# Attention and a squared-ReLU feed-forward block on one core: both feed-forward products as seven block products instead of eight

## The chip, the core and the metric

The kernel runs on one core of a Trainium2 chip. The metric is device time in microseconds (us) of one execution. A run gives one time, and its profile gives the span of the core, which lies some 2 us below it. In profile lines PE is TensorE's matmul side, PEld its weight loads, DVE VectorE, ACT ScalarE, POOL GpSimd and SP SyncE, which issues most transfers here. `L84` is line 84 of the kernel that was run, so the same operation has other line numbers in another kernel.

## The reference, cut to what matters

```python
# q, k, v: (8 batches, 8 heads, 576 positions, 64), float32; g_norm: (64,)
kv  = np.einsum('bhsd,bhse->bhde', k, v)          # one 64x64 matrix a head
out = np.einsum('bhsd,bhde->bhse', q, kv)
rms = np.sqrt(np.mean(out * out, axis=-1, keepdims=True) + 1e-06)
x   = (out / rms * g_norm)                        # -> (4608 tokens, 512)

h = x @ w_in                                      # w_in:  (512, 2048)
r = np.maximum(h, 0.0)
g = s * (r * r) + b                               # s, b: scalars
return (g @ w_out).astype(np.float32)             # w_out: (2048, 512)
```

Both weights arrive as 8-byte floats, because they are float32 arrays multiplied by a numpy scalar of 8 bytes. The kernel has to bring them to 4 bytes itself. K and V of a pair of batches are needed before any of its tokens can be worked on. There are four pairs of batches.

## The kernel before

It works in 12 tiles of 384 tokens. The weights are loaded in 32 blocks of 128x512, each converted by nine operations on three engines, and stay in on-chip memory. A tile has 16x4 first products, 384 columns wide, and 3x16 second ones, 512 wide. The attention of the next tile stands between first products, one step behind each. K and V are loaded for two heads at a time and multiplied between second products.

```python
    def round_w(i):                    # 8-byte words -> float32, one block of 512
        raw = w_raw.pop(i).rearrange("p (n two) -> p n two", two=2)
        lo, hi = raw[:, :, 0], raw[:, :, 1]
        ...
        nc.vector.tensor_scalar(out=m, in0=hi, scalar1=0xFFFFF, ...)           # mantissa
        nc.vector.tensor_scalar(out=e, in0=hi, scalar1=20, scalar2=0x7FF, ...)  # exponent
        nc.scalar.activation(l, lo, AF.Copy, scale=2.0**-52)
        nc.scalar.activation(one_m, m, AF.Copy, bias=1.0, scale=2.0**-20)
        nc.vector.tensor_scalar(out=e, in0=e, scalar1=896.0, scalar2=1151.0, ...)
        nc.vector.tensor_scalar(out=e, in0=e, scalar1=896.0, scalar2=2.0**23, ...)
        nc.vector.scalar_tensor_tensor(e, hi, 0x80000000, e, ...)
        nc.gpsimd.tensor_tensor(out=one_m, in0=one_m, in1=l, op=ALU.add)
        nc.gpsimd.tensor_tensor(out=w_sb[i], in0=one_m, in1=e.bitcast(FP32), op=ALU.mult)

    def mm1(T, f):
        h = ps_h.tile([P, N], FP32, name="h_ps", tag="h")
        for c in range(KC):
            nc.tensor.matmul(
                h, lhsT=w_in(c, f), rhs=xT[T][:, c, :], start=(c == 0), stop=(c == KC - 1)
            )
        ...                            # relu on ScalarE, square and s*r^2+b on VectorE

    def mm2(T, j):
        o = ps_o.tile([P, DM], FP32, name="o_ps", tag="o")
        for f in range(FC):
            nc.tensor.matmul(o, lhsT=gT[T, f][:, j * P : j * P + P], rhs=w_out(f), ...)
        ...                            # copied and stored

    # main loop, cut
    for T in range(NT):
        ...
        for f in range(FC):
            if T == 0:
                w_step(f + 2)          # converts a block, loads a later one
            mm1(T, f)
            if f < len(steps):
                steps[f]()             # attention of the next tile
        if T == 0:
            for i in range(FC + 2, 2 * FC):
                w_step(i)              # most of w_out
            ...
        for j in range(J):
            mm2(T, j)
            ...                        # kv_product of the next pair of batches
```

## Time and profile before

| | before |
|---|---|
| time, median of three runs | 1276.54 us (1275.0 to 1276.94) |
| span of the profiled run | 1273.7 us |
| TensorE busy | 1141.2 us, 90% |
| VectorE busy | 408.3 us, 32% |
| end of the first tile | 245.21 us |
| a later tile without K/V products | 92.75 us |

The busy row and the slices (40 equal parts of the span, each digit a busy share in tenths) are shown in the prediction. TensorE is full from the eighth slice on, so the kernel has two parts: a first tile that is held by the conversion of the weights, and eleven tiles that are held by TensorE. In the timeline the columns are start, length and what ran, and in brackets the wait before it. In rows of the page, as the prediction shows them, what stands behind the last bar is idle time before such an instruction, with the instruction that ended it.

```profile
171.56 2.08 PE L294 MATMUL o_ps<-w,gT 128*128 128x512 f32 x2 [2.29 <-POOL w L148]
...
215.19 30.18 PE L294 MATMUL o_ps<-w,gT 128*128 128x512 f32 x66 [2.20 <-POOL w L148]
245.21 2.74 PE L277 MATMUL h_ps<-xT,w 128*128 128x384 f32 x8
```

The second product of the first tile waits some 2.3 us for each block that GpSimd delivers, and GpSimd in turn waits for VectorE's `w_e` (1.62 us here). VectorE has next to no idle time, but its queue is not long by its work alone. Of its 160 conversion operations in the timeline, the 113 that run beside nothing of GpSimd's for more than 0.34 us take at most 0.69 us. The other 47, like the two shown, overlap a GpSimd operation by 1.08 us or more and take 1.37 to 1.67. At the short durations the 125.4 us of VectorE's conversion would be about 76 (an estimate: 32 blocks of 0.42, 0.42, 0.43, 0.43 and 0.69 us). So some 49 us go with running beside GpSimd. That is read from this trace; no run takes GpSimd away by itself.

### The profile page before, as it was taken

The page shows a single profiled execution, that of the slowest core. Times are in us where ns is not written, and L with a number is a line of the kernel's source. Part 1 is how long each engine was busy: PE and PEld are TensorE (multiplying, and loading weights), DVE is VectorE, ACT ScalarE, POOL GpSimd, SP SyncE. Part 2 cuts the span into 40 slices and gives each one's busy share as a digit, 9 for nine tenths or more (in the row PEclk, how much of TensorE's full clock was granted, in tenths as well). Part 3 has the DMA queues.
Part 4 walks back from the last instruction along what each step waited for, and adds up shares of the span by engine and source line. Part 5 has one row for each costly group of instructions (what it writes and reads, how often), then busy time and mean ns, then how long its engine had stood idle before and what let it go on. Part 6 is the DMA issues. An engine that isn't in the chain of part 4 may idle for free.

```text
span 1273.7 us, 11355 instructions
## 1 busy us (share of the span) xinstructions
PE 1141.2 (90%) x4704; PEld 600.7 (47%) x4704; DVE 408.3 (32%) x697; ACT 208.8 (16%) x409; POOL 90.6 (7%) x72
## 2 busy tenths in 40 slices
PE   3576645989999989999989999999999999999998
PEld 3343311455554454454554454454554554554553
DVE  0599996041141041141141141140240140240220
ACT  0233321021021020120120120120120120120110
POOL 0244564000000000000000000000000000000000
PEclk9988755999999999999999999999999999999999
DMA  9223235001620000001610000001410000000000
GB/s 230 51 83 100 97 118 152 21 1 46 146 58 9 16 1 9 17 1 46 170 33 9 17 1 8 17 1 46 105 25 8 17 1 9 16 1 17 9 0 25
DMA packets 63668, 55.27 MB, mean 43 GB/s; under 512 B 40576, under 2 KB 48768, under 8 KB 63616
## 3 DMA queue, kind: packets, MB, share of 16 engines
q1 hardware_dynamic: 57984, 45.10, 14.0%
q10 hardware_dynamic: 5632, 9.44, 2.0%
q8 instruction: 37, 0.61, 0.2%
q14 instruction: 15, 0.12, 0.0%
HBM read 45.09 MB, written 9.44 MB: 43 GB/s over the span
## 4 chain that ended last, share of the span: by engine, by line
PE 75%; DVE 17%; issue 6%; ACT 2%; POOL 0%; POOLq 0%; DVEq 0%
PE o_ps L294 38%; PE h_ps L277 31%; DVE gT L285 3%; PE x_ps L236 2%; DVE w_e L141 2%; DVE w_e L138 2%; DVE r L283 2%; DVE w_e L132 2%; DVE xn L255 2%; DVE ss L249 2%; PE xT_ps L262 2%; ACT r L281 1%; PE kv_ps L196 1%; PE qT_ps L227 1%; DVE w_e L144 1%
## 5 line engine op out<-in xcount | busy, mean ns | idle before, releaser
L294 PE MATMUL o_ps<-w,gT 128*128 128x512 f32 x1152 | 517.0, 608 | 37.8 <-POOL w L148 37.8
L277 PE MATMUL h_ps<-xT,w 128*128 128x384 f32 x1536 | 533.0, 499 | 9.9 <-POOL w L148 9.9
L277 PEld LDWEIGHTS h_ps<-xT,w 128*128 128x128 f32 x1536 | 290.2, 195 | 202.2 <-issue 22.1
L294 PEld LDWEIGHTS o_ps<-w,gT 128*128 128x128 f32 x1152 | 220.6, 194 | 325.4 <-issue 260.2
L283 DVE TENSOR_TENSOR r<-r 128x384 f32<-128x384 f32 x192 | 106.7, 556 | 616.2 <-ACT r L281 616.1
L281 ACT ACTIVATE r<-h_ps 128x384 f32<-128x384 f32 x192 | 93.9, 489 | 354.3 <-PE h_ps L277 337.0
L285 DVE TENSOR_SCALAR gT<-r,s_col,b_col 128x384 f32<-128x384 f32 x192 | 105.6, 550 | 7.9
L302 ACT COPY o_sb<-o_ps 128x512 f32<-128x512 f32 x36 | 21.1, 585 | 477.2 <-PE o_ps L294 477.2
L262 PE MATMUL xT_ps<-ident,xn 128*128 128x128 f32 x144 | 26.3, 311 | 53.9 <-DVE xn L255 53.9
L209 DVE COPY bd_kv<-kv_ps 64x256 f32<-64x256 f32 x8 | 3.4, 423 | 163.5 <-PE kv_ps L196 163.5
L262 PEld LDWEIGHTS xT_ps<-ident,xn 128*128 128x128 f32 x144 | 16.9, 153 | 75.3 <-DVE xn L255 68.8
L147 POOL TENSOR_TENSOR w_1m<-w_1m,w_l 128x512 f32<-128x512 f32 x32 | 43.7, 1366 | 82.3 <-ACT w_1m L137 82.3
L236 PE MATMUL x_ps<-bd_kv,qT 128*64 128x128 f32 x576 | 42.0, 291 | 6.8 <-DVE qT L229 6.8
L148 POOL TENSOR_TENSOR w<-w_1m,w_e 128x512 f32<-128x512 f32 x32 | 45.0, 1405 | 41.6 <-DVE w_e L144 40.0
L236 PEld LDWEIGHTS x_ps<-bd_kv,qT 128*64 128x64 f32 x576 | 32.9, 144 | 26.1 <-issue 16.0
L196 PE MATMUL kv_ps<-v_sb,k_sb 64*64 64x64 f32 x1152 | 25.3, 244 | 19.6 <-DMA v_sb<-in_v_dram 19.6
L196 PEld LDWEIGHTS kv_ps<-v_sb,k_sb 64*64 64x64 f32 x1152 | 22.7, 156 | 27.6 <-issue 22.7
L137 ACT ACTIVATE w_1m<-w_m 128x512 f32<-128x512 uint32 x32 | 20.2, 630 | 92.2 <-DVE w_m L129 92.2
L141 DVE TENSOR_SCALAR w_e<-w_e 128x512 uint32<-128x512 uint32 x32 | 32.2, 1005 | 1.1
L265 ACT ACTIVATE xT<-xT_ps,g_col 128x512 f32<-128x512 f32 x36 | 24.7, 686 | 42.1 <-PE xT_ps L262 42.1
L132 DVE TENSOR_SCALAR w_e<-w_raw 128x512 uint32<-128x512 uint32 x32 | 28.8, 901 | 0.0
L138 DVE TENSOR_SCALAR w_e<-w_e 128x512 uint32<-128x512 uint32 x32 | 26.9, 841 | 1.1
(21 smaller groups left out, 221.6 us busy)
## 6 DMA issues: line engine op xcount, KB each, us to landing
k_sb<-in_k_dram SPq DMA_DIRECT2D x32, 288.0 KB, 4.7
v_sb<-in_v_dram SPq DMA_DIRECT2D x32, 288.0 KB, 5.9
q_sb<-in_q_dram SPq DMA_DIRECT2D x72, 128.0 KB, 3.3
out_dram<-o_sb ACTq DMA_DIRECT2D x36, 256.0 KB, 2.0
w_raw<-in_moe_w_in_dram SPq DMA_DIRECT2D x16, 512.0 KB, 3.7
w_raw<-in_moe_w_out_dram SPq DMA_DIRECT2D x16, 512.0 KB, 3.2
g_col<-in_g_norm_dram ACTq DMA_DIRECT2D x2, 0.2 KB, 3.0
s_col<-in_moe_s_dram ACTq DMA_DIRECT2D x1, 0.5 KB, 5.5
```

The source lines that it names most:

```text
L132: nc.vector.tensor_scalar(out=e, in0=hi, scalar1=20, scalar2=0x7FF, op0=ALU.logical_shift_right, op1=ALU.bitwise_and,)
L138: nc.vector.tensor_scalar(out=e, in0=e, scalar1=896.0, scalar2=1151.0, op0=ALU.max, op1=ALU.min)
L141: nc.vector.tensor_scalar(out=e, in0=e, scalar1=896.0, scalar2=2.0**23, op0=ALU.subtract, op1=ALU.mult)
L148: nc.gpsimd.tensor_tensor(out=w_sb[i], in0=one_m, in1=e.bitcast(FP32), op=ALU.mult)
L196: nc.tensor.matmul(kv_ps[g][s][l * HB : l * HB + HB, p, :], lhsT=kt[rows, l, j, :], rhs=vt[rows, l, j, :], start=(j == 0), stop=(j == R - 1),)
L236: nc.tensor.matmul(st["x"][half, p, :], lhsT=st["qT"][:, p, half], rhs=bd[:, s, p, :], start=True, stop=True,)
L262: nc.tensor.transpose(ps[:, p, :], st["xn"][:, 2 * p : 2 * p + 2, :], ident)
L277: nc.tensor.matmul(h, lhsT=w_in(c, f), rhs=xT[T][:, c, :], start=(c == 0), stop=(c == KC - 1))
L281: nc.scalar.activation(r, h, AF.Relu)
L283: nc.vector.tensor_mul(r2, r, r)
L285: nc.vector.tensor_scalar(out=gT[T, f], in0=r2, scalar1=s_col, scalar2=b_col, op0=ALU.mult, op1=ALU.add)
L294: nc.tensor.matmul(o, lhsT=gT[T, f][:, j * P : j * P + P], rhs=w_out(f), start=(f == 0), stop=(f == FC - 1),)
```

## The change

Its intent is to do seven eighths of the multiplications. A 2x2 block product needs eight block multiplications, or seven with sums of blocks before and after (Strassen's scheme, in a form with few sums). In the new kernel:

- A unit is 512 tokens, so there are 9 units. Both dimensions that are cut in half on each side give 256-column instructions instead of 384 or 512.
- The first product runs in four strips of hidden units. A strip has seven block products of four matmuls. Several of them accumulate into one PSUM bank, and the state in the middle is copied out by ScalarE (`keep`).
- The second product has 14 block products of eight matmuls. The sums of w_out's blocks are not kept on chip: its seven operands, 1 MB each, are made once, **stored to device memory** and streamed back in every unit through a ring of three buffers.
- The conversion of the weights is new: two multiplications on ScalarE, then a shift, a three-operand step and one integer add on VectorE, and nothing on GpSimd.
- `b` is taken out of `g` and comes back as a row, `b` times the column sums of w_out, in the output.
- K and V are loaded one head at a time, and the four head pairs of a pair of batches are multiplied in one run, in the second half of a unit.

The diff, cut to its core (cuts marked "..."; the sums of x, the other block products and the loads are left out):

```diff
-    J = 3
-    TPG = R // J
-    N = J * P
+    TB = 2 * P
+    U = CH // 4
+    NS = FC // 4
...
+        nc.scalar.activation(hi, hi, AF.Copy, scale=2.0**-112)
+        nc.scalar.activation(lo, lo, AF.Copy, scale=2.0**-29)
+        yb, db = raw.rearrange("p (n two) -> p n two", two=2)[:, :, 1], dst.bitcast(U32)
         nc.vector.tensor_scalar(
...
+            out=db, in0=yb, scalar1=3, scalar2=0x7FFFFFFF,
+            op0=ALU.logical_shift_left, op1=ALU.bitwise_and,
         )
         nc.vector.scalar_tensor_tensor(
-            e, hi, 0x80000000, e, ALU.bitwise_and, ALU.bitwise_or
+            db, yb, 0x80000000, db, ALU.bitwise_and, ALU.bitwise_or
         )
-        nc.gpsimd.tensor_tensor(out=one_m, in0=one_m, in1=l, op=ALU.add)
-        nc.gpsimd.tensor_tensor(out=w_sb[i], in0=one_m, in1=e.bitcast(FP32), op=ALU.mult)
+        nc.vector.tensor_tensor(out=db, in0=db, in1=lo, op=ALU.add)
...
+    def make_w_out(s):
+        up = convp.tile([P, 2, DM], FP32, name="w_up", tag="up")
+        dn = convp.tile([P, 2, DM], FP32, name="w_dn", tag="dn")
+        t = convp.tile([P, 3, 2, HN], FP32, name="w_t", tag="wt")
+        round_w(FC + 2 * s, up)
+        round_w(FC + FC // 2 + 2 * s, dn)
...
+        sub(t1, b12, b11)
...                                         # four column sums into wsum
+        sub(t3, b22, b12)
+        sub(t2, b22, t1)
+        sub(t4, b21, t2)
+        for i, src in ((1, b11), (2, b21), (6, t2), (7, t3), (5, t1), (3, b22), (4, t4)):
+            nc.sync.dma_start(out=w2_dram[i][:, 2 * s : 2 * s + 2, :], in_=src)
...
+        def keep(name, src):
+            st[name] = rp.tile([P, 2, TB], FP32, name=name, tag=name)
+            nc.scalar.copy(st[name], src)
+
+        def x1():
+            st["x"] = bank_of("x", "x")
+            mm1_product(1, u, s, st["x"], True)
+            keep("r1", st["x"])
...
+        def x6():
+            mm1_product(6, u, s, st["x"], False)
+            keep("r2", st["x"])
...
+        def product(i, j, ps, first):
+            for f in range(FC // 2):
+                s, b = divmod(f, 2)
+                matmul(
+                    ps, ga[G_OF[i], s][:, b, j * P : j * P + P], ring[u, i][:, f, :],
+                    first and f == 0, f == FC // 2 - 1,
+                )
...
+            if c % R == 0:
+                todo.append([lambda p=p, g=c // R: kv_product(g, p) for p in range(NP)])
+            todo += [[a] for a in attention(c)]
...
+            if u == 0 and n == m1:
+                for s in range(NS):
+                    make_w_out(s)
+                    send_w()
+                    send_w()
+                tc_late()
+                bias_row()
+                load_w2(0, 0)
+                load_w2(0, 1)
...
+                for m, step in enumerate(todo[done]):
+                    step()
+                    if len(todo[done]) > 1 and m < 2:
+                        for h in (4 + 2 * m, 5 + 2 * m):
+                            load_kv(kv_due[u], h)
```

## The prediction

> **What bounds the kernel now.** I read the page first: busy shares, the 40 slices, then the groups of instructions.
>
> ```profile
> PE 1141.2 (90%) x4704; PEld 600.7 (47%) x4704; DVE 408.3 (32%) x697; ACT 208.8 (16%) x409; POOL 90.6 (7%) x72
> ...
> PE   3576645989999989999989999999999999999998
> ...
> DVE  0599996041141041141141141140240140240220
> ...
> PEclk9988755999999999999999999999999999999999
> ...
> L294 PE MATMUL o_ps<-w,gT 128*128 128x512 f32 x1152 | 517.0, 608 | 37.8 <-POOL w L148 37.8
> L277 PE MATMUL h_ps<-xT,w 128*128 128x384 f32 x1536 | 533.0, 499 | 9.9 <-POOL w L148 9.9
> ```
>
> Two stages show. From slice 8 TensorE is full at full clock and VectorE mostly idle. In slices 3 to 7 VectorE is full or nearly so and TensorE half empty, its clock falling to 5 tenths: the conversion of the 8-byte weights. So TensorE bounds the last 1030 us, the conversion what is before.
>
> There are 12 tiles of 384 tokens: 12x16x4 = 768 first products and 36x16 = 576 second ones. The rows count twice that, so an fp32 product is two instructions. Their means (608, 499) overlap each other; the timeline of TensorE gives the true spacing (start, length, what):
>
> ```profile
> 384.28 10.49 PE L277 MATMUL h_ps<-xT,w 128*128 128x384 f32 x32
> 394.60 41.36 PE L294 MATMUL o_ps<-w,gT 128*128 128x512 f32 x96
> 435.80 2.74 PE L277 MATMUL h_ps<-xT,w 128*128 128x384 f32 x8
> ```
>
> (394.60-384.28)/32 = 322.5 ns for 384 columns, (435.80-394.60)/96 = 429.2 for 512: 0.833 ns a column plus 2.5 ns. The products make 12 x (128x0.3225 + 96x0.4292) = 990 us. This tile began at 343.05 in the same view, so it took 92.75 us, 82.5 of it products; 10.25 is the attention of three chunks of 128 tokens, 3.4 us each, of which 1.07 is a wait for VectorE before the second transpose. At the front the same view has the first tile ending at 245.21, so 245.21 - 92.75 = 152 us is not steady work.
>
> **What the Trainium skill says.** "TensorE: Matmul & The Clock Gate", Part 2 (step by step), says the weights of the next matmul load while this one runs, in a time set by their columns, 128/1.2 = 107 ns. The trace agrees with the overlap: a load is recorded at 190 ns (median), yet both shapes leave only 2.5 ns between matmuls. Part 1 there says a pause of some 3.4 us halves the clock; the trace agrees: at 160 to 200 us, products after waits of 2.30 us are 19.20 of 40 us at a granted 0.50. "VectorE: DVE Perf Modes", the TRN2 errata section, gives an fp32 two-tensor operation of N elements (N+151)/0.96 ns. For 512 that is 691, and the trace has 692 for xn. "PSUM — Partial Sum Buffer", The four PSUM rules, allows a synchronised read in the middle of an accumulation group; the changed kernel does this throughout, and no run here shows it.
>
> **Products.** Strassen needs seven block products for eight. Per unit of 512 tokens the first side is 4 strips x 7 x 4 fp32 products, the second 7 x 2 x 8: 224 products, 448 instructions, each of 256 columns. By the line above each takes 213.3+2.5 = 215.8 ns, above the 190 of a weight load, so loads stay hidden: 96.7 us a unit, 9 x 96.7 = **870 us**, 120 less than 990. (7/8 of 990 would be 866; the shorter instruction loses 4.)
>
> **Attention.** Four chunks go in front (below), 32 beside second products. Each is 1.96 us of matmuls in the timeline (0.44, 1.03, 0.49) plus some 0.5 for waits, as its steps now stand a whole second product (3.45 us) apart: 32 x 2.5 = **80 us**, against 33 x 3.4 = 112.
>
> **Sums on VectorE.** A strip has 9 operations of 512 elements, 9 x 0.69 = 6.2 us against 7x8x0.2158 = 12.1 of products. A unit's second half has 14 small ones, 8 of 512 and the attention's, some 20 of 58 us. Both hidden. The seven 1 MB operands of a unit come in over some 58 us with three buffers, 13 us ahead; at the speed below one takes 4.5. Hidden too.
>
> **K and V.** This I read from the order of the built program: for the second to fourth pair of batches all four head pairs are multiplied in one run, with buffers for the first two. The loads of the other two start only when the first products free them. The windows give what the queue moves (the last two columns, DMA share and GB/s):
>
> ```profile
> 18.00:22.00 4.00, 0.17 (x2) 0.21 (x2) 0.00 (x0) 0.00 (x0) 0.00 (x0) 1.00 1.04 238
> 328.00:332.00 4.00, 4.00 (x10) 1.71 (x9) 0.00 (x0) 0.00 (x0) 0.00 (x0) 1.00 0.92 228
> ```
>
> Two heads of K and V are 1.18 MB, 5.1 us at 232 GB/s, the next two 5.1 more, and 2 of latency: 12.2 us, of which 1.2 is hidden. So 1.2 for the first head pair, 12.2, 1.2 for the last, and about 1.8 for a clock gone cold (a pair takes 2.2 us in the first stage, 1.2 later): 16.4 us instead of 4.9, 3 x 16.4 = **49 us**.
>
> **Front.** Two blocks of weights (2 MB, 9 us at that speed) now load ahead of K and V, so the K/V products end near 33 (30.2 before). ScalarE copies and converts until 40, VectorE converts until 47 (11 us, below) and only then serves the norm. Four chunks chained through one PSUM bank at 5.9 us: the products start at **69** (59 before).
>
> **First products of the first unit.** A pair of blocks of w_in is converted per strip. Each block of 1024 elements has a shift (0.68, from 0.42 for 512), a three-operand step (1.22), and an integer add that the order shows as one instruction of 2048 half-words (an estimate by the same formula, 2.29): 4.2 us, two are 8.4, and four sums 2.8: 11.2. With the 6.2 of the strip VectorE needs 17.4 us where TensorE needs 12.1, for three of four strips, part of it absorbed. Followed by hand, the strips take 58 us instead of 48.3: **+10**, at 127.
>
> **The conversion of w_out.** The new second product needs all of w_out, because each operand is stored to device memory and read back. Until then TensorE has nothing: the attention of the next unit also stands behind. A quarter is 8.4 + 5.5 (eight sums) = 13.9 us of VectorE. Its stores stand ahead of the next raw load in one queue, and the last waits for the last sum; so store, load (1 MB for the first block) and ScalarE's step come after it, 2.5 + 7 + 1.1: 24.5 us a quarter. 2 + 13.9 + 3x24.5 + 9 (stores land, first operand read) = **99 us** with TensorE idle, from 127 to 226. This is the largest term against the change.
>
> Sum: 69 + 10 + 99 + 870 + 80 + 49 + 4 (last sum and store) + 5 (small waits, cold clock) = 1186 of span; measured times lie 3 us above it (1276.54 and 1273.7): **1190 us**, 7% less.
>
> **Rivals.** (a) The 256-column instruction does not hide its load, say 240 ns: 4032 x 24 = 97 us more, 1285, the same. For it: 190 recorded leaves only 26 of room. Against: in the timeline sixteen of the attention's instructions take 1.03 us, 64 ns each, though the page records their loads at 144, so a record is longer than what a load holds up. (b) The first stage is well hidden and the gain is nearly the whole 120 plus attention's 30: near 1110. Against it is the order: nothing stands beside w_out's conversion. (c) The mid-group copies, in one queue on ScalarE with one product (1.73 us) of room, hold up TensorE by 0.3 us in each strip product: 252 x 0.3 = 76 us, 1265. A copy takes 0.585, so there is room for two. (d) Streaming operands stall second products. It needs below 150 GB/s, and 228 was reached beside matmuls.
>
> **Range and chances.** w_out's stage is good to 15 us, front and first strips to 12, K/V to 12, small waits in 63 steady strips and products to 15: together about 28, so 1155 to 1230 with some weight above. Over 2% faster means below 1251; only (a) or (c) gets there: 0.93 faster, 0.06 same, 0.01 slower.
>
> **What would show it.** Matmuls of 256 columns spaced 215.8 ns in the timeline, 4032 of them; a unit near 107 us; TensorE empty some 100 us around 127 to 226 with VectorE in bursts of 14 and DMA between; three gaps of about 11 us inside K/V products; first products at 69. It is wrong if spacing exceeds 225, if the idle stretch is below 80 or above 120, or if waits for ScalarE copies recur in every strip.

## More of the kernel before

Lines of the timeline, of VectorE and GpSimd first and then of TensorE, show how the first part runs and ends.

```profile
161.42 1.34 POOL L148 TENSOR_TENSOR w<-w_1m,w_e 128x512 f32<-128x512 f32 x1 [1.62 <-DVE w_e L144]
161.53 1.52 DVE L132 TENSOR_SCALAR w_e<-w_raw 128x512 uint32<-128x512 uint32 x1
...
162.73 1.44 POOL L147 TENSOR_TENSOR w_1m<-w_1m,w_l 128x512 f32<-128x512 f32 x1
...
163.09 1.37 DVE L138 TENSOR_SCALAR w_e<-w_e 128x512 uint32<-128x512 uint32 x1
```

## The result, and the profile after

The changed kernel is correct and takes **1180.21 us** (median of four runs, 1175.63 to 1181.61; the kernel before in the same rounds 1276.22, 1275.0 to 1276.94). The ratio is 0.9242 with a 95% interval of 0.9216 to 0.9268. A ratio here is the mean time of one kernel's fast runs over that of the other's fast runs of the same rounds, so it is not quite the ratio of the medians. The profiled run is of 1181.61 us, its span 1179.8 us.

The page's busy row and its slices:

```profile
PE 1010.7 (86%) x6050; PEld 869.3 (74%) x6050; DVE 480.9 (41%) x765; ACT 203.4 (17%) x338; POOL 2.5 (0%) x8
...
PE   2588100799978999999979999998699999999998
...
DVE  0469565234431355244414452443044534433541
...
DMA  7434445336133401270245023602350234034022
```

Slices are counted from 0 here; each is 29.5 us. Of VectorE's four nines (slices 2 to 5 before) one is left. In their place TensorE has a hole in slices 4 to 6, and there VectorE is only half busy: a chain, no longer a full engine. Three smaller dents follow, at slices 11, 20 and 27 to 28: the K/V runs. Between them TensorE is full. Rows of the page, and the windows view of one undisturbed unit (columns after the window: length, then busy time of PE, PEld, DVE, ACT and POOL with their counts, granted clock, DMA share, GB/s):

```profile
L84 PE MATMUL x_ps<-w_sb,a 128*128 128x256 f32 x864 | 200.6, 386 | 9.7 <-DMA w_sb<-w 9.7
...
L374 ACT COPY r<-x_ps 128x512 f32<-128x512 f32 x108 | 63.2, 585 | 343.7 <-PE x_ps L84 338.8
```

```profile
402.93:508.52 105.59, 105.32 (x545) 91.25 (x544) 44.48 (x74) 17.98 (x32) 0.00 (x0) 1.00 0.27 90
```

Streamed operands (`w_sb`) cost 9.7 us once, before the very first of them, and nothing later. The copies out of the middle of a group are 585 ns each, and no matmul row of the page names them as what it waited for. The undisturbed unit has TensorE busy for 105.32 of 105.59 us, at full clock.

The spacing of the new instruction is read in TensorE's timeline where block products of eight instructions follow each other without a gap (ten such lines are left out at the dots):

```profile
402.94 1.89 PE L84 MATMUL x_ps<-xT,wa 128*128 128x256 f32 x8
...
421.93 1.89 PE L84 MATMUL x_ps<-xs,ws 128*128 128x256 f32 x8
```

From the first line to the last are 11 products of eight instructions, so (421.93 - 402.94)/88 = 215.8 ns each, as the prediction had it. The hole, in the same view and then with all engines and the transfer queue (`SPq` is the issue of transfers):

```profile
121.57 1.89 PE L84 MATMUL x_ps<-xs,ws 128*128 128x256 f32 x8
201.37 2.07 PE L84 MATMUL b_ps<-wsum,b_sq 128*128 128x512 f32 x2 [77.91 <-DVE wsum L161]
213.13 6.56 PE L84 MATMUL x_ps<-w_sb,a 128*128 128x256 f32 x16 [9.69 <-DMA w_sb<-w]
```

```profile
127.59 1.23 DVE L158 CUSTOM_DVE_ANT_0 w_up<-w_raw,w_up 128x2048 uint16<-128x2048 uint16 x1
...
135.68 1.41 DVE L164 TENSOR_TENSOR w_t<-w_dn,w_t 128x512 f32<-128x512 f32 x2
...
138.99 2.29 SPq L130 DMA_DIRECT2D w_raw<-in_moe_w_out_dram  x4
146.19 1.14 ACT L148 ACTIVATE w_raw<-w_raw 128x1024 f32<-128x1024 f32 x1 [17.94 <-DMA w_raw<-in_moe_w_out_dram]
...
147.36 0.69 DVE L151 TENSOR_SCALAR w_up<-w_raw 128x1024 uint32<-128x1024 uint32 x1 [10.27 <-ACT w_raw L148]
```

These five lines are one quarter of w_out. VectorE finishes the last sum at 137.09, the next raw load is issued only at 138.99, after all seven stores, ScalarE starts on what arrived at 146.19, and VectorE goes on at 147.36. VectorE's first step of a quarter falls at 147.36, 169.35 and 191.39, so a quarter takes 22.0 us, and 10.27 of them VectorE waits for this step alone (in all it is busy for 11.37 of 21.99).

A K/V run, in TensorE's timeline and the queue's:

```profile
341.62 2.58 PE L262 MATMUL kv_ps<-v_sb,k_sb 64*64 64x64 f32 x144
347.92 0.33 PE L262 MATMUL kv_ps<-v_sb,k_sb 64*64 64x64 f32 x2 [3.72 <-DMA v_sb<-in_v_dram]
...
358.18 2.15 PE L262 MATMUL kv_ps<-v_sb,k_sb 64*64 64x64 f32 x66 [1.82 <-DMA v_sb<-in_v_dram]
360.26 2.07 PE L84 MATMUL x_ps<-w_sb,a 128*128 128x256 f32 x4
```

```profile
342.93 1.11 SPq L93 DMA_DIRECT2D k_sb<-in_k_dram  x2
```

The first two head pairs (144 instructions) run in 2.58 us from what was loaded early. The loads of the other two are issued from 342.93 on, when the first pair has freed a buffer: sixteen transfers, the last of which is issued by 354.29, with nothing else between them in that queue. The last of them lets TensorE go on at 358.18. The run takes 360.26 - 341.62 = 18.6 us.

### The profile page after: what moved, and what is told of

Same layout as the page of the kernel before. It is cut to its first block, busy times and chain, and to the rows that moved or that the text cites. A ratio compares the mean times of both kernels' runs of the same rounds, so it can differ in the third digit from the quotient of the medians.

```text
span 1179.8 us, 14111 instructions
## 1 busy us (share of the span) xinstructions
PE 1010.7 (86%) x6050; PEld 869.3 (74%) x6050; DVE 480.9 (41%) x765; ACT 203.4 (17%) x338; POOL 2.5 (0%) x8
## 4 chain that ended last, share of the span: by engine, by line
PE 76%; DVE 10%; SPq 5%; DMA 5%; issue 2%; ACT 2%; DVEq 0%; ACTq 0%
PE x_ps L84 42%; PE y_ps L84 23%; PE z_ps L84 5%; SPq L93 4%; PE x_ps L295 3%; PE xT_ps L320 2%; DVE a L164 2%; DMA w_raw<-in_moe_w_out_dram 2%; PE qT_ps L286 1%; DMA v_sb<-in_v_dram 1%; PE kv_ps L262 1%; DVE wsum L161 1%; DVE xn L312 1%; SPq L220 1%; DVE ss L306 1%
## 5 line engine op out<-in xcount | busy, mean ns | idle before, releaser
L84 PE MATMUL x_ps<-w_sb,a 128*128 128x256 f32 x864 | 200.6, 386 | 9.7 <-DMA w_sb<-w 9.7
L84 PEld LDWEIGHTS x_ps<-w_sb,a 128*128 128x128 f32 x864 | 164.3, 193 | 35.6 <-issue 13.8
L84 PE MATMUL y_ps<-w_sb,a 128*128 128x256 f32 x720 | 162.5, 381 | 0.0
L84 PEld LDWEIGHTS y_ps<-w_sb,a 128*128 128x128 f32 x720 | 135.1, 191 | 17.5 <-issue 0.2
L84 PE MATMUL y_ps<-xs,wb 128*128 128x256 f32 x576 | 136.4, 380 | 0.7 <-DVE a L161 0.7
L84 PE MATMUL x_ps<-xs,ws 128*128 128x256 f32 x576 | 136.2, 379 | 0.0
L84 PEld LDWEIGHTS x_ps<-xs,ws 128*128 128x128 f32 x576 | 109.4, 190 | 15.2 <-ACT r L374 0.4
L84 PEld LDWEIGHTS y_ps<-xs,wb 128*128 128x128 f32 x576 | 109.0, 191 | 15.6 <-DVE a L161 1.1
L362 DVE SCALAR_TENSOR_TENSOR a<-a 128x512 f32<-128x512 f32 x108 | 74.7, 692 | 3.7
L84 PE MATMUL z_ps<-xT,wa 128*128 128x256 f32 x288 | 70.1, 387 | 4.5 <-DVE a L161 4.5
L84 PE MATMUL x_ps<-xT,wa 128*128 128x256 f32 x288 | 69.6, 385 | 0.0
```

The source lines that it names most:

```text
L84: nc.tensor.matmul(o, lhsT=lhsT, rhs=rhs, start=start, stop=stop, skip_group_check=True)
L362: nc.vector.scalar_tensor_tensor(t, t, 0.0, t, ALU.max, ALU.mult)
```

## The experiments

All eleven kernels gave correct results and were timed in three rounds beside the kernel before (median 1276.5 to 1276.8 us in each set), four runs each. Each is faster than the kernel before by far more than its interval, so the question is by how much.

The **theory** is the prediction's ledger: each part of it is to be removed by itself. The **rivals** were that another cost, not named in it, sets the time (spacing, copies, streaming), and that the gain is not Strassen's at all.

### 1. The kernel before with only the new conversion

The change bundles two things. This takes the second alone: the kernel before, with `round_w` replaced.

```diff
-        nc.gpsimd.tensor_tensor(out=one_m, in0=one_m, in1=l, op=ALU.add)
-        nc.gpsimd.tensor_tensor(out=w_sb[i], in0=one_m, in1=e.bitcast(FP32), op=ALU.mult)
+        nc.scalar.activation(hi, hi, AF.Copy, scale=2.0**-112)
+        nc.scalar.activation(lo, lo, AF.Copy, scale=2.0**-29)
...                                  # shift, three-operand step
+        nc.vector.tensor_tensor(out=db, in0=db, in1=lo, op=ALU.add)
```

> The kernel before with nothing but the new rounding of the 8-byte weights (two ScalarE, three VectorE operations, no GpSimd). Theory A: a good part of the gain is not Strassen's but this cheaper conversion. VectorE then needs about 1.8 us a block of 512 instead of some 4.4 to 5.2, the first tile of 384 tokens ends near 165 us instead of 245, the steady tiles stay at 92.75, and the time is near 1196 us. Theory B: the gain is Strassen's; the conversion is hidden for the most part, and the time stays above 1250 us.

Measured: **1206.92 us**, ratio 0.9455 (0.9441 to 0.9469). Its slices and the end of its first tile:

```profile
PE   3498799999999999999999999899999999999998
...
DVE  0389604204303402402411411410420430430320
```

```profile
147.22 28.59 PE L283 MATMUL o_ps<-w,gT 128*128 128x512 f32 x66 [1.54 <-DVE w L137]
175.65 2.74 PE L266 MATMUL h_ps<-xT,w 128*128 128x384 f32 x8
```

The first tile ends at 175.65 instead of 245.21, so 69.6 us, and that is the whole gain of 1276.5 - 1206.9 = 69.6. A later tile without K/V products takes 92.75 us (273.49 to 366.24), as before. So 70 of the 96 us that the full change gains are the conversion's, and everything else together brings 26.7. Theory A was right in kind and missed by 10 us (it had the first tile end at 165 and the time at 1196); where these 10 us lie was not followed up. VectorE's shift, which now has no GpSimd operation beside it, takes 421 ns in all 32 blocks.

### 2. K/V products spread, each ahead of its loads' need

The K/V products leave the run in the second half and go between strip products of the first half, one pair at a time, each pair of loads being issued as soon as a buffer is free.

```diff
-            if c % R == 0:
-                todo.append([lambda p=p, g=c // R: kv_product(g, p) for p in range(NP)])
...
+            if u in kv_due and n in (8, 11, 17, 21):
+                p = (8, 11, 17, 21).index(n)
+                kv_product(kv_due[u], p)
+                if p < 2:
+                    for h in (4 + 2 * p, 5 + 2 * p):
+                        load_kv(kv_due[u], h)
```

> The changed kernel with the K/V products of the second to fourth pair of batches moved from one run in the second half of a unit to four places in its first half, two or more block products apart. Theory A: the three long units (126.2, 124.2, 129.9 us) are long by 63.5 us only because the run waits for loads that it itself releases; spread, each costs its own 4.9 us of matmuls, units become 110.5 us, and the time falls by 49 us to about 1131. Theory B: the loads are what is short, and the wait turns up again at the spread products or at the operands of the second product: above 1160 us.

Measured: **1136.54 us**, ratio 0.8907 (0.8892 to 0.8922), 44 us less than the changed kernel. The second pair's products, in TensorE's timeline:

```profile
297.19 1.28 PE L262 MATMUL kv_ps<-v_sb,k_sb 64*64 64x64 f32 x72
```

72 instructions take 1.28 us with no wait. The first pair still waits for its loads (0.64 and 0.69 us). The three units with K/V take 113.11, 112.60 and 111.49 us, where 110.5 were expected, and are 20.4 us over an undisturbed unit in sum where they were 63.5 over. So the run's waits for loads that it releases itself were what made these units long. The edit does two things at once, though: it spreads the run, and it moves the loads into the half of a unit in which no operand is streamed. No run separates the two.

### 3. The raw loads of w_out ahead of the stores

```diff
         sub(t4, b21, t2)
+        send_w()
+        send_w()
         for i, src in ((1, b11), (2, b21), (6, t2), (7, t3), (5, t1), (3, b22), (4, t4)):
             nc.sync.dma_start(out=w2_dram[i][:, 2 * s : 2 * s + 2, :], in_=src)
...
                     make_w_out(s)
-                    send_w()
-                    send_w()
```

> The changed kernel with the next quarter's raw w_out loads put ahead of this quarter's stores in the queue. Theory A: the 22.0 us of a quarter are 11.4 of VectorE and 10.6 of waiting for loads that stand behind stores; with the loads ahead they run beside the sums and a quarter takes about 15 us (VectorE then waits for the stores of its single buffers), TensorE's idle stretch falls from 90 to about 69 us, and the time to about 1159. Theory B: the queue's volume is the bound (2.1 MB in and 1.8 MB out a quarter), a quarter stays at 20 us or more, and the time above 1172.

Measured: **1159.42 us**, ratio 0.9081 (0.9068 to 0.9095), 20.8 us less than the changed kernel. The issue of the raw loads, and TensorE's wait:

```profile
127.20 4.03 SPq L130 DMA_DIRECT2D w_raw<-in_moe_w_out_dram  x4
```

```profile
180.84 2.07 PE L84 MATMUL b_ps<-wsum,b_sq 128*128 128x512 f32 x2 [59.02 <-DVE wsum L161]
```

The loads go out at 127.20 instead of 138.99, and the wait is 59.02 instead of 77.91, which is 18.9 of the 20.8 us. The Trainium skill, "DMA: Bandwidth & Descriptors", section "Anatomy of one DMA — SWDGE (gpsimd) path", says that transfer engines do not wait on semaphores: the issuing sequencer does, before dispatch. Here SyncE issues: a store whose sum is not ready holds the loads behind it in that sequencer (138.99 against 127.20). In the first quarter the loads went out 17.4 us after the last strip product had started (121.57), now 7.3 (119.93 in this run), so some 10 us were lost to the order. A quarter is now 15.4 to 15.9 us (VectorE's first steps at 123.86, 139.25, 155.01 and 170.86), still over VectorE's own 11.4: that first step now waits 3.8 to 4.0 us for a store out of the single buffers. The transfers are hardly faster. They move up to 368 GB/s here, and the changed kernel itself reaches 325 in the same stage (windows view, 142 to 146 us). What changed is that the loads now run beside VectorE's sums and not after them.

### 4 and 5. Strassen's scheme on the first product only

Here the second product is the plain one, 512 columns wide, with w_out resident and nothing stored or streamed.

```diff
-        for i, src in ((1, b11), (2, b21), (6, t2), (7, t3), (5, t1), (3, b22), (4, t4)):
-            nc.sync.dma_start(out=w2_dram[i][:, 2 * s : 2 * s + 2, :], in_=src)
+        for half in range(2):
+            t = wp.tile([P, 2, DM], FP32, name=f"wo_{half}_{s}")
+            round_w(FC + half * (FC // 2) + 2 * s, t)
+            wo[half, s] = t
...
+                    matmul(
+                        st[c], g[:, b, j * P : j * P + P], wo[half, s][:, b],
+                        s == 0 and half == 0 and b == 0, s == NS - 1 and half == 1 and b == 1,
+                    )
```

> Strassen on the first product alone: the second is plain, 512 columns wide, from a w_out that stays on chip, with no operands stored and read back. Theory A: the second product's Strassen saves 9 x 6.6 = 59 us of matmuls and costs nearly all of the 90 us in which TensorE waits for its operands; plain, units take 112.2 us instead of 105.6, but the first unit ends near 206 us instead of 277, and the time is about 1163, below the changed kernel. Theory B: the conversion of w_out holds up TensorE as long without the stores: about 1235 us.

Measured: **1191.73 us**, ratio 0.9335 (0.9318 to 0.9353): a miss, and through faults of the experiment. To make room, single buffers had been given to the kept copies, so TensorE waited for ScalarE (7.75 and 5.72 us), and the column sums stood before the first output and held it for 11.21 us. A third wait for ScalarE, 0.73 us in each of the nine units, has another cause: with the slots changed, the last strip's `x3` follows `x5` directly, with no product between them to cover the copy. The run says nothing about the question. It was built again with two buffers for two of the three kept copies (the transposed q and the normalised x made single for that), and with the sums and the first output later. The wait of some 0.7 us a unit stayed:

> first_only again without its two faults, which its trace shows: single buffers for two kept partial sums (TensorE waited 7.8, 5.7 and eight times 0.7 us for ScalarE copies) and the column sums of w_out in front of the first output (TensorE waited 11.2 us for them). Theory A: that is what put it at 1191.7 instead of 1163; now the first unit ends near 203 us, units take 112 us, and the time is 1151 us, some 29 below the changed kernel: Strassen on the second product, as built, costs more than it saves. Theory B: the plain second product is as slow for another cause: above 1175.

Measured: **1170.79 us**, ratio 0.917 (0.9148 to 0.9192). That lies between the two expectations. Its undisturbed units take 112.62 us, as expected (7.04 over 105.59: 64 second products of 0.858 us instead of 112 of 0.432, 6.6 us by the spacings; the rest is of the size of the 0.68 us for which the copy that no product covers holds TensorE). But the first unit ended at 215.97 instead of 203:

```profile
129.09 6.61 PE L84 MATMUL x_ps<-wo,a 128*128 128x512 f32 x8 [5.13 <-DVE wo L158]
...
151.00 5.92 PE L84 MATMUL x_ps<-wo,a 128*128 128x512 f32 x8 [6.11 <-DVE wo L158]
```

The second product waits for each pair of converted blocks. The quarters came 9.5 to 12.5 us apart, not the 6.3 that VectorE needs for two blocks. In the trace ScalarE's first step waits for the transfer at one place (5.34 us) and stands behind the attention's own operations at another, and no run separates the two. Against the changed kernel the first unit is 60.8 us shorter, the seven middle units and the last are 7x7.04 + 7.6 = 56.9 longer, and K/V runs 10 shorter. So **Strassen's scheme on the second product, as built, is a wash**: what it saves in eight units it spends on its operands in the first. The other 10 us suggest that the streamed operands lengthen the K/V runs in the shared queue (their excess here is 17.4, 17.7 and 18.1 us, against 20.6, 18.6 and 24.3), but that is a comparison and not an isolated run.

### 6 and 7. The mends together

The sixth kernel joins experiments 2 and 3 and moves the column sums of w_out from VectorE to TensorE, which was idle there (`b_sq` transposed times each block, accumulated in one PSUM bank).

```diff
-        for m, b in ((up, 0), (up, 1), (dn, 0), (dn, 1)):
-            if (s, b) != (0, 0) or m is dn:
-                add(wsum, wsum, m[:, b])
+            late["b"] = ps_t.tile([P, DM], FP32, name="b_ps", tag="t")
+        for n, (m, b) in enumerate(((up, 0), (up, 1), (dn, 0), (dn, 1))):
+            matmul(late["b"], b_sq, m[:, b], s == 0 and n == 0, s == NS - 1 and n == 3)
```

> kv_spread and loads_ahead together, and the column sums of w_out (4 x 2.8 us of VectorE) made by TensorE, which is idle then. If the three are independent, the 43.7 us of the first, the 20.8 of the second and 11 more add up: 1104 us, and a quarter of w_out takes 13 us instead of 15.7. If stores are what a quarter waits for, the sums on TensorE give nothing: 1115 us.

Measured: **1115.61 us**, ratio 0.8739 (0.8726 to 0.8752). Experiments 2 and 3 added up would make 1136.5 - 20.8 = 1115.7 (no run has those two alone), so taking four operations a quarter off VectorE gave nothing. A quarter still takes 15.6 to 15.7 us: VectorE's first step only waits longer for the store out of its single output buffer, 6.3 to 6.5 us where it was 3.8 to 4.0 in experiment 3. The seventh kernel gives those buffers two (and makes room with a single one for the transposed q and for the normalised x):

```diff
-        up = convp.tile([P, 2, DM], FP32, name="w_up", tag="up")
-        dn = convp.tile([P, 2, DM], FP32, name="w_dn", tag="dn")
+        up = convp.tile([P, 2, DM], FP32, name="w_up", tag="up", bufs=2)
+        dn = convp.tile([P, 2, DM], FP32, name="w_dn", tag="dn", bufs=2)
```

> three_mends with two buffers each for the two rounded blocks of w_out, so that rounding need not wait for the stores of the quarter before. If those stores hold it up, a quarter falls from about 13 to 9 us of VectorE, or to some 11 or 12 that the queue needs for 3.9 MB at the 306 to 368 GB/s seen in the trace: 1100 us, 3 to 6 below three_mends. If the raw loads hold it up, no difference.

Measured: **1102.21 us**, ratio 0.8632 (0.8619 to 0.8645). The quarters are now 9.5, 12.3 and 11.3 us. The same step of VectorE, in the sixth kernel and then in the seventh:

```profile
140.59 0.69 DVE L151 TENSOR_SCALAR w_up<-w_raw 128x1024 uint32<-128x1024 uint32 x1 [6.45 <-DMA w<-w_t]
```

```profile
134.36 0.69 DVE L151 TENSOR_SCALAR w_up<-w_raw 128x1024 uint32<-128x1024 uint32 x1 [0.27 <-ACT w_raw L148]
```

The wait for the store is gone: the single buffers were it. The gain was 13.4 us where 3 to 6 were expected; the time was right only because experiment 6 had come in late.

### 8. A ring of two

```diff
-        late["ring"] = ctx.enter_context(tc.tile_pool(name="ringp", bufs=3, side="right"))
+        late["ring"] = ctx.enter_context(tc.tile_pool(name="ringp", bufs=2, side="right"))
```

> The changed kernel with two buffers instead of three for the streamed operands of the second product: each 1 MB load may then start only one product (6.9 to 8.9 us) ahead. Theory A: streaming is hidden with room (a load lands in 4.9 us), so the time stays within 5 us of the changed kernel's, 1180. Theory B: three buffers are what hides it; each of 63 loads then delays TensorE by 1 us or more: above 1240.

Measured: **1175.83 us**, ratio 0.9215 (0.92 to 0.9231). One buffer less for the streamed operands costs nothing. An operand lands 4.9 us after its issue, and its two products take 6.9 us. Streaming is hidden with room to spare, and rival (d) of the prediction is refuted.

### 9. Every copy out of the middle of a group done twice

```diff
             nc.scalar.copy(st[name], src)
+            nc.scalar.copy(st[name], src)
```

> The changed kernel with every copy of a partial sum by ScalarE made twice: 108 more copies of 0.585 us in the middle of accumulation groups. Theory A: the order of the block products leaves each copy at least one product of 1.73 us, so a second one fits: steady units stay at 105.6 us and the time within 5 us of 1180. Theory B: these copies stand in TensorE's way; 7 of 12 a unit follow with one product of room, and a doubled one costs 0.6 us in some of them: 15 us or more.

Measured: **1179.13 us**, ratio 0.9234 (0.9219 to 0.9249), so no change. Both copies are in the trace (count, then shortest, median and longest in ns, and first and last start):

```profile
L374 ACT COPY r<-x_ps x108: 579/585/589, 71.8 to 1124.5; 128x512 f32<-128x512 f32 x108
L375 ACT COPY r<-x_ps x108: 585/585/590, 72.4 to 1125.1; 128x512 f32<-128x512 f32 x108
```

Rival (c) is refuted for this kernel: a block product of 1.73 us covers even two copies of 0.585 us, and the unit stayed at 105.59 us. Where no product covers the copy, it does show, at 0.68 us (experiment 5).

### 10. The first strip's conversion ahead of the K/V products in program order

On top of the seventh kernel. VectorE and ScalarE then convert while K and V still load, and serve the norm as soon as it comes.

```diff
+    make_w_in(0)
     for p in range(NP):
         kv_product(0, p)
-    make_w_in(0)
```

> four_mends with the first pair of w_in blocks converted before the first K/V products in program order, not after. Theory A: in the front the norm of the first chunk waits for VectorE, which converts from 38 to 48 us although the raw weights have been there since 12; converted early, the first block products start near 60 us instead of 67.7: 1094 us. Theory B: the K/V loads set the front, and they are not earlier: less than 3 us.

Measured: **1094.27 us**, ratio 0.8569 (0.8554 to 0.8583). It is the best version, and beats both kernels. The same transpose of the first stage, first in the changed kernel and then in this one, with this one's first block product:

```profile
50.36 1.12 PE L320 MATMUL xT_ps<-ident,xn 128*128 128x128 f32 x4 [4.50 <-DVE xn L312]
```

```profile
44.21 1.12 PE L319 MATMUL xT_ps<-ident,xn 128*128 128x128 f32 x4 [1.73 <-DVE xn L311]
...
60.95 3.62 PE L84 MATMUL x_ps<-xT,wa 128*128 128x256 f32 x8
```

The wait for VectorE's `xn` falls from 4.50 to 1.73 us, and the block products start at 60.95 instead of 67.7 in the seventh kernel. The page of this version has TensorE at 93%, and one dent left at slices 4 to 6:

```profile
PE 1015.2 (93%) x6080; PEld 862.2 (79%) x6080; DVE 471.5 (43%) x749; ACT 203.4 (19%) x338; POOL 2.5 (0%) x8
...
PE   2588647999999999999999999999999999999998
```

### 11. Strassen on the first product only, with the K/V mend

Experiment 5 found the second side a wash as built. Is it still one when its stage is mended? This is kernel 5 with the edit of experiment 2, to be set against the seventh kernel.

> first_only2 with kv_spread's places for the K/V products. Its three long units (53.3 us over the others) fall to three times 6: 1135 us. Set against four_mends (1102), which has the same mend and both products by Strassen with w_out's stage shortened, this tells whether Strassen on the second product pays once its stage is mended: theory A says by 57 us in the later units less what is left of the stage (first unit 172 us there, 148 here), about 33 us; theory B, that it never pays, needs 1102 or less here.

Measured: **1132.94 us**, ratio 0.8869 (0.8856 to 0.8883), against 1102.21. So the second side is worth 31 us once its loads, stores and buffers are in order. 6.1 of the 31 us are this kernel's own waits for ScalarE that experiment 5 left in. The mends of w_out's stage have no counterpart here either: the first unit still has the slow quarters of experiment 5, though it ends at 215.72 against 239.89 in the seventh kernel. How much of the 31 us would go or come if these were mended too is open.

## Why the prediction was right

The time came within 10 us of the prediction, but by a sum whose terms partly cancel: w_out's stage and the units were sized too large by 9.3 and 7.7 us, K/V too small by 14.5. That the total came so close is partly luck. In the profiled span (1179.8 us; predicted 1186):

| step of the prediction | predicted | measured | where |
|---|---|---|---|
| start to first block product | 69 | 68.6 | first matmul of 256 columns at 68.58 |
| first products of unit 1 | 58 | 58.3 | 68.58 to 123.46, and the last two products, 3.5 together, behind the hole |
| TensorE without work for w_out | 99 | 89.7 | 123.46 to 213.13 |
| rest of unit 1 | 58.4 | 60.2 | 213.13 to 276.77 less the 3.5 |
| seven units, K/V aside | 7 x 106.7 | 7 x 105.6 | 402.93 to 508.52 |
| K/V, three times | 49 | 63.5 | 20.6 + 18.6 + 24.3 over 105.59 |
| last unit, with last store | 100.7 | 100.4 | 1079.36 to the end |
| small waits | 5 | none seen apart | |

The predicted parts of units are 96.7 us of products and 2.5 for each of four chunks of attention; the last unit has no attention.

**Products.** Right to the last digit: 215.8 ns, loads hidden. Rival (a) needed 240.

**Attention.** A chunk took (105.59 - 96.7)/4 = 2.2 us instead of 2.5. Its steps, a whole block product apart, left next to no waits.

**The conversion of w_out.** The mechanism was right, the size 9 us too large. The mis-sized term is the integer add, which the prediction sized by half-words at 2.29 us. It took 1.23, about half. VectorE's part of a quarter is 11.4 us instead of 13.9, 2.1 of the difference by the two adds, and a quarter is 22.0 instead of 24.5. Experiments 3, 6 and 7 show the rest of the step: queue order first, then the single buffers, and VectorE last.

**K and V.** The mechanism was right (experiment 2), the size 14.5 us too small: "12.2 us" for the last two pairs. In the run shown above the loads were issued from 342.93 on and TensorE went on at 358.18, so 15.3 us. The sixteen transfers took until 354.29 to be issued alone, 11.4 us, where the prediction had 10.2 for moving the data, and TensorE went on 3.9 us later, where it had 2. They are loads of one head each, 0.59 us to issue, where the kernel before spends 0.60 us on one of two heads. The third run also has a wait of 2.85 us for the norm before it.

The 3 us between span and time came of two different runs, too: in one run they are 1.8 (1181.61 and 1179.8).

**What it did not ask.** Its rival (b), "the first stage is well hidden", was wrong for the kernel as built. But the time near 1110 that it named was within reach of short edits to queue order and buffers: experiments 7 and 10 have 1102 and 1094 us. And it set the whole gain against "120 less" of products, without asking what the new conversion would do for the kernel before. Experiment 1 gives that split. From there to the changed kernel, in spans: a token costs 92.7/384 = 0.2414 us there and 105.59/512 = 0.2062 after, times 4096 tokens makes 144 us saved. Of these about 106 are products ((82.5/384 - 96.7/512) x 4096), the rest the attention, whose steps stand further apart. The first unit gives back 276.77 - 175.65 - 128x0.2414 = 70.2. K/V give back 63.5 less three times 5.1 (97.84 - 92.75, a tile with and without K/V products), so 48.2. That leaves 25.7; measured, 1204.5 - 1179.8 = 24.7. So the saving of the steady units was there nearly in full, the attention's part included, and four fifths of the 144 us were spent on getting Strassen's operands in place and on a loading order.

## What to carry to other kernels

When a change bundles a new algorithm with a cheaper preparation, give the preparation to the old kernel first: here it alone was worth 70 of the 96 us. A scheme that saves an eighth of the multiplications pays only if its operands are ready without a stop; read the order of the transfer queue, where a store that is not ready holds every load behind it, give what is stored a second buffer, and see to it that a load's buffer comes free well before its data are needed. An engine that looks full may be slowed by its neighbour: compare the shortest and the longest of one operation before believing its busy share. Size a chain by its waits: taking work off an engine inside it (experiment 6) does nothing while a transfer is what the chain waits for.

## What the Trainium skill lacked or had wrong

- "FP8 and Floating Point Precision", TensorE Precision Notes, says that true fp32 takes four passes. The runs show how this is issued and what it costs: two instructions, each 0.833 ns a column and 2.5 ns on top, at 215.8, 322.5 and 429.2 ns for 256, 384 and 512 columns. A page with a table of this would have saved the working, since a narrower fp32 product loses only its 2.5 ns.
- "VectorE: DVE Perf Modes" does not say by which of its rows an integer add goes that the trace records as a custom operation on 2048 half-words. It takes 1224 to 1226 ns. The fp32 formula, which the prediction took, gives 2291 for 2048 elements; the page's perf-mode tier table has 1224 for a 16-bit two-tensor operation of 2048, which fits.
- "PSUM — Partial Sum Buffer", The four PSUM rules, allows a synchronised read in the middle of an accumulation group and gives no cost. With 108 such copies, or with each done twice, the time is the same (1180.2 and 1179.1 us). In experiments 4 and 5, where no product stands between the copy and the next accumulation into that bank, it held TensorE for 0.7 us.
